# The last two products of the last output tile, computed in two halves of 128 columns, and another order of the last steps

## The chip, the cores and the metric

The kernel runs on one core of a Trainium2 chip. The metric is the device time of one execution in microseconds, and the number that counts is the median of several executions. Beside it stands one execution taken by the hardware profiler, on which all statements about single instructions rest. Engines are named as the profile names them: PE is the matrix engine, PEld its weight loads, DVE the vector engine, ACT the scalar engine, POOL the GpSimd engine, SP the sync engine, which here only issues DMAs and waits.

## The reference

The computation has two stages. The first is block-wise attention: a small 8x8 matrix per head is normalised by five rounds of exponential, row and column scaling, blocks of keys and values are mixed with it, and softmax attention runs inside each block of 96 positions. The second stage is a maxout layer over the 3072 tokens, and this is the one that the change touches:

```python
x  = attn_out.transpose(0, 2, 1, 3).reshape(B * S, H * D)   # 3072 x 512
h1 = x @ w1                                                  # 512 -> 1024
h2 = x @ w2
g  = maximum(h1, h2)
out = g @ w_out                                              # 1024 -> 512, float32
```

There are 4 batches of 768 tokens.

## The kernel before, in words

The kernel uses max(h1, h2) = relu(h1 - h2) + h2. So it computes g = relu(x(w1 - w2)) and then out = g w_out + x (w2 w_out), where w2 w_out is made once and kept as `wc`. The output product therefore contracts over 1024 rows of g and 512 rows of x, 12 blocks of 128 in all.

That output product is computed by the scheme that multiplies 2x2 blocks with seven products instead of eight. The two row blocks are the two halves of a batch (`ch` 0 and 1, 384 tokens each), the two column blocks are the two halves of the 512 output columns (`NW` = 256), and the two contraction blocks are the two halves of g and of x. Each of the seven products contracts over 6 blocks of 128. One class, `Group` (L932), holds what belongs together: a P group handles two tiles of 128 tokens of each half of the batch, a U group the third tile. A step of a P group is 12 matmuls of 128x128 weights by 256 columns, a step of a U group 6 of them.

The seven steps of a group (`step`, L1047, and `chain`, L1008) work on two banks of one PSUM buffer. Step 0 makes A11 B11 in bank 0 and copies it out. Step 1 makes A12 B21 in bank 1 and adds the copy: that is the first quarter of the output. Step 2 goes on adding to bank 0 and copies to the place of the quarter (ch 1, first columns); step 3 goes on in bank 0 and copies to the place of the quarter (ch 1, last columns); step 4 finishes bank 0 and copies it to the quarter (ch 0, last columns). Step 5 starts anew in bank 1 and adds its result to what step 3 left; step 6 goes on in the same bank 1 and adds to what step 2 left. `add` (L981) does a sum on DVE, `copy` (L992) a copy on DVE or ACT, `product` (L956) issues the matmuls, and `store` (L999) sends finished columns to the output. `send` (L1028) says what is stored after which step; after step 4 it is all of ch 0, after step 5 the last columns of ch 1, after step 6 of the last batch the first columns of ch 1, through ACT's queue.

Nothing here is scheduled by a planner. The order is a list of words written out by hand (L1176 to L1204), and each word is one step: `P3.5D` is step 5 of the P group of batch 3, with its sum on DVE, `U3.4A` step 4 of the U group with its copy on ACT, `O1.3.6` the store that follows step 6 of the U group (O0 is the P group). Each engine works through its own instructions in that order, and waits on counters (semaphores) for those of other engines. Reads of one bank do not hold up matmuls into the other bank, which `apart` (L941) declares.

DMAs issued by SP and ACT use eight completion semaphores in turn, numbered 0 to 7. At the end of the program SP waits for all of them, one instruction after another, in the order 0 to 7; then the engines meet at a barrier and the program ends. Before the change, the last store (`O1.3.6`, on ACT's queue) has semaphore 7, and SP's wait for it is the last of its nine.

Of the kernel before, what the change touches and what calls it, by code (L numbers as in the profile page):

```python
# [16 lines left out]
def kernel(  # L17
# [16 lines left out]
    nc = tc.nc  # L34
    AF = mybir.ActivationFunctionType
    ALU = mybir.AluOpType
    AX = mybir.AxisListType

    B, H, S, D = q.shape
# [14 lines left out]
    NW = DMODEL // 2  # L54
# [854 lines left out]
    def left(b, which, k, off):  # L909
        c = slice(off, off + 128)  # L910
        if k < 4:
            t, m = divmod(k, 2)
            if which in (1, 2, 4):
                return sums_g[:, {1: 0, 2: 1, 4: 2}[which], k, c]
            ch, t = {"a11": (0, t), "a12": (0, t + 2), "a22": (1, t + 2), 3: (1, t)}[which]
            return g_tiles[b, ch, t][:, m, c]
        j = k - 4
        if which in (1, 2, 3, 4):
            return sums_x[:, which - 1, j, c]
        ch, half = {"a11": (0, 0), "a12": (0, 1), "a22": (1, 1)}[which]  # L920
        return xT[:, b % 2, ch, j, half, c]

    def right(which, k):
        if which in (1, 2, 3, 4):
            if k >= 4:
                return wt_c[:, which - 1, k - 4]
            return (wt_early if which in (1, 3) else wt_late)[:, (which - 1) // 2, k]
        half, n = {"b11": (0, 0), "b21": (1, 0), "b22": (1, 1)}[which]
        n = slice(n * NW, (n + 1) * NW)
        return wo_sb[:, half * 4 + k, n] if k < 4 else wc[:, half * 2 + k - 4, n]  # L930

    class Group:  # L932
# [66 lines left out]
        def store(self, ch, c0=0, c1=DMODEL, queue=nc.sync):  # L999
# [5 lines left out]
                in_=self.o[ch][:, :, c0:c1],  # L1005
            )

        def chain(self, at, eng):  # L1008
            if at == 1:
                self.product(1, "a12", "b21", True)  # L1010
                self.add(0, 0, 1, self.by_tile(self.a), [self.first], eng)
            elif at == 2:
                self.product(0, 2, 2, False)
                self.second = self.copy(self.part(1, 0), 0, eng)
            elif at == 3:
                self.product(0, 1, 1, False)
                self.third = self.copy(self.part(1, 1), 0, eng)
            elif at == 4:
                self.product(0, 4, "b22", False)
                self.copy(self.part(0, 1), 0, eng)  # L1020
            elif at == 5:
                self.product(1, 3, 3, True)
                self.add(1, 1, 1, self.part(1, 1), [self.third], eng)
            else:
                self.product(1, "a22", 4, False)
                self.add(1, 0, 1, self.part(1, 0), [self.second], eng)

        def send(self, at):  # L1028

            last = self.b == B - 1  # L1030
            if at == 4:
                self.store(0)
            elif at == 5:
                self.store(1, NW)
            elif last:
                self.store(1, 0, NW, nc.scalar)
            elif len(self.tiles) > 1:
                self.store(1)
            else:
                nc.sync.dma_start(  # L1040
                    out=out[self.b * S : (self.b + 1) * S, :].rearrange(
                        "(c t p) n -> p c t n", c=2, p=128
                    )[:, :, self.tiles[0], :],
                    in_=self.both,
                )
# [35 lines left out]
    def token(text):  # L1081
# [117 lines left out]
        P2.3A x3.2 v3.6 U2.4D U2.6D x3.3 Y3.1.0D Y3.0.0D Y3.1.1D P2.5D P2.4A X3.1D X3.2D X3.3D P2.6D  # L1199
        Y3.0.2D Y3.1.2A X3.4D Y3.0.1D O1.2.6 Y3.0.3A O0.2.4 Y3.1.3D Y3.1.5A Y3.0.5D Y3.1.4A Y3.0.4A  # L1200
        Y3.1.6D Y3.0.6D U3.0A P3.0A G3.1.1D G3.0.1D G3.0.2D G3.1.2D O0.2.6 P3.1D G3.0.4D G3.0.3D
        G3.1.4D P3.2A G3.1.3D U3.1D U3.2A P3.3D P3.5D P3.4A P3.6D U3.3D U3.5D O0.3.5 O0.3.4 O0.3.6
        O1.3.5 U3.4A U3.6D O1.3.6 O1.3.4
        """,  # L1204
    ]
    for part in plan:
# [30 lines left out]
```

## Time and profile before

| what | us |
|---|---|
| median of 3 executions | 156.07 |
| lowest and highest | 155.84, 156.44 |
| the profiled execution's own time | 156.11 |
| its span, first to last instruction | 154.3 |
| outside the span | 1.8 |

The page of the profile gives busy times by engine, the span in 40 slices, the chain of work that ended last, the costliest groups of instructions and the DMAs. Where the text goes to single instructions it uses the timeline, whose rows give the start, the busy time from the first to the last of the merged instructions, engine, line, operation, output and inputs, shapes, and the count; the brackets at the end give the idle time of the engine before them and what ended it. A DMA that SP or ACT issues stands there with the time that the issue took; the time from issue to landing stands in the list of DMAs. The row of a group of matmuls ends when the last one has run through the array, which is later than the moment when the next matmul can start.

### The profile page before, as it was taken

How to read it: one execution, taken by the hardware profiler on the slowest of the kernel's cores; microseconds unless marked ns; L12 is line 12 of the kernel's file. 1: busy time of each engine (PE TensorE's matmuls, PEld its weight loads, DVE VectorE, ACT ScalarE, POOL GpSimd, SP SyncE). 2: the span in 40 equal slices, each digit the busy share in tenths (PEclk: the TensorE clock that was granted, in tenths of full speed). 3: DMA queues.
4: the chain of work that ended last, by engine and by line, in shares of the span. 5: the costliest groups of instructions: out<-in, count | busy, mean ns of one | idle time of the engine just before them, and what ended most of it. 6: DMA issues, size and time to landing. Idle time of an engine off the chain costs nothing.

```text
span 154.3 us, 5157 instructions
## 1 busy us (share of the span) xinstructions
PE 147.4 (96%) x2238; PEld 114.0 (74%) x2238; DVE 134.7 (87%) x287; ACT 102.0 (66%) x134; POOL 25.3 (16%) x53
## 2 busy tenths in 40 slices
PE   6999989999999999999999999989999999999991
PEld 6948867555678788887567998765688978578881
DVE  4888989999999999986999999658899999999731
ACT  3488897268899997879859797888792301463010
POOL 7999541100210400001500000000000000000000
PEclk9999999999999999999999999999999999999999
DMA  3999999999999972998999939996001475500065
GB/s 45 197 207 197 197 204 207 217 215 215 216 215 199 205 155 57 150 133 219 287 205 211 188 62 150 165 195 253 0 4 24 85 116 203 187 6 0 0 224 184
DMA packets 28918, 23.93 MB, mean 155 GB/s; under 512 B 16672, under 2 KB 24608, under 8 KB 28896
## 3 DMA queue, kind: packets, MB, share of 16 engines
q0 software_dynamic: 9280, 13.37, 49.1%
q1 hardware_dynamic: 19200, 9.84, 28.9%
q10 hardware_dynamic: 416, 0.39, 0.8%
q8 instruction: 17, 0.28, 0.7%
q14 instruction: 5, 0.04, 0.1%
HBM read 26.75 MB, written 6.29 MB: 214 GB/s over the span
## 4 chain that ended last, share of the span: by engine, by line
PE 62%; DVE 24%; ACT 4%; DMA 3%; issue 3%; DVEq 0%
PE out_ps L961 32%; PE hb_ps L805 10%; PE hq_ps L805 8%; PE o_ps L612 4%; DVE g L824 4%; DVE x L629 3%; PE k_ps L489 3%; PE s_ps L584 3%; DMA xT<-x 2%; ACT kT L109 2%; DVE w_sb L771 2%; PE v_ps L554 1%; DVE v_dc L255 1%; DVE sums_x L891 1%; DVE w_sb L236 1%
## 5 line engine op out<-in xcount | busy, mean ns | idle before, releaser
L805 PEld LDWEIGHTS <-w_sb 128*128 128x128 bf16 x224 | 21.5, 98 | 14.7 <-issue 0.8
L599 ACT ACTIVATE e<-s_ps 96x768 bf16<-96x768 f32 x32 | 24.1, 807 | 2.2 <-PE s_ps L584 2.0
L629 DVE TENSOR_TENSOR x<-o_ps,rs 96x512 bf16<-96x512 f32 x32 | 22.0, 686 | 1.1
L996 ACT COPY o<-out_ps 128x512 f32<-128x512 f32 (+1 forms) x18 | 8.6, 479 | 21.5 <-PE out_ps L961 21.2
L961 PEld LDWEIGHTS <-g 128*128 128x128 bf16 x192 | 18.2, 98 | 2.4
L805 PE MATMUL hb_ps<-sums_x,w_sb 128*128 128x384 bf16 x96 | 18.2, 327 | 0.0
L961 PEld LDWEIGHTS <-sums_g 128*128 128x128 bf16 x144 | 13.5, 97 | 2.2 <-issue 0.2
L961 PE MATMUL out_ps<-wo_sb,g 128*128 128x256 bf16 x96 | 13.1, 273 | 0.0
L987 DVE TENSOR_TENSOR o<-out_ps,o 128x512 f32<-128x512 f32 (+1 forms) x16 | 8.9, 553 | 4.7 <-PE out_ps L961 4.6
L109 ACT CAST kT<-k_ps 128x1024 bf16<-128x1024 f32 x12 | 11.6, 1020 | 2.0 <-PE k_ps L489 2.0
L805 PE MATMUL hq_ps<-xT,w_sb 128*128 128x384 bf16 x64 | 12.7, 326 | 0.0
L612 PE MATMUL o_ps<-v_sb,e 96*128 96x65 bf16 x256 | 12.4, 194 | 0.0
L612 PEld LDWEIGHTS <-e 96*128 96x128 bf16 x256 | 10.7, 98 | 1.5 <-DVE x L629 0.2
L961 PE MATMUL out_ps<-w2T,sums_x 128*128 128x256 bf16 x72 | 11.8, 273 | 0.0
L584 PE MATMUL s_ps<-qT,kT 64*128 64x96 bf16 x256 | 9.2, 204 | 1.1 <-ACT qT L109 0.7
L111 DVE CAST v_sb<-v_ps 96x1024 bf16<-96x1024 f32 x8 | 9.6, 1214 | 0.2 <-PE v_ps L531 0.2
L961 PEld LDWEIGHTS <-sums_x 128*128 128x128 bf16 x96 | 8.6, 97 | 1.2
L584 PEld LDWEIGHTS <-kT 64*128 64x128 bf16 x256 | 6.4, 94 | 3.5 <-issue 2.6
L826 ACT ACTIVATE g<-g 128x768 bf16<-128x768 bf16 x7 | 5.9, 842 | 4.4 <-DVE g L824 4.4
L83 PE MATMUL fill_ps<-fill 128*128 128x118 bf16 x92 | 7.3, 264 | 1.2 <-DVE fill L74 1.2
L176 POOL DMA_DIRECT2D v_raw<-in_v_dram x11 | 6.5, 597 | 11.2 <-DVE v_dc L255 4.3
L109 ACT CAST v_sb<-v_ps 96x1024 bf16<-96x1024 f32 x8 | 7.8, 1016 | 0.6 <-PE v_ps L554 0.6
(129 smaller groups left out, 304.2 us busy)
## 6 DMA issues: line engine op xcount, KB each, us to landing
out_dram<-o SPq DMA_DIRECT2D x10, 512.0 KB, 2.9
v_raw<-in_v_dram POOLq DMA_DIRECT2D x8, 384.0 KB, 16.2
k_raw<-in_k_dram POOLq DMA_DIRECT2D x3, 768.0 KB, 10.8
w_sb<-in_moe_w_dram POOLq DMA_DIRECT2D x4, 256.0 KB, 7.6
wo_sb<-in_moe_w_out_dram POOLq DMA_DIRECT2D x2, 512.0 KB, 11.2
w_sb<-in_moe_w_dram POOLq DMA_DIRECT2D x2, 512.0 KB, 14.8
v_raw<-in_v_dram POOLq DMA_DIRECT2D x3, 256.0 KB, 4.7
k_raw<-in_k_dram POOLq DMA_DIRECT2D x3, 256.0 KB, 6.4
```

The source lines that it names most:

```text
L83: nc.tensor.matmul(ps[:, 0:w], w0, fill[:, 0:w], start=True, stop=True)
L109: nc.scalar.copy(out=out_ap, in_=in_ap)
L111: nc.vector.tensor_copy(out=out_ap, in_=in_ap)
L176: nc.gpsimd.dma_start(out=v_raw[r0 : r0 + 64, m * n : (m + 1) * n], in_=v_src[b, :, m * n : (m + 1) * n],)
L584: nc.tensor.matmul(ps[:, h2 * 512 + ii * 128 : h2 * 512 + ii * 128 + BLK], kT[b][rows, (hp * 8 + i) * BLK : (hp * 8 + i) * BLK + 128], rhs ...
L599: nc.scalar.activation(out=e_out, in_=src, func=AF.Exp, scale=scale)
L612: nc.tensor.matmul(ps[:, h2 * 512 + ii * 65 : h2 * 512 + (ii + 1) * 65], e[:, (h2 * 4 + ii) * BLK : (h2 * 4 + ii) * BLK + 128], v_sb[:, m0 ...
L629: nc.vector.tensor_tensor(out=x, in0=ov[:, :, :, 0:D], in1=rs.to_broadcast([BLK, 2, 4, D]), op=ALU.mult,)
L805: nc.tensor.matmul(ps[:, m * 512 : m * 512 + TCH], w[:, k, c : c + 128], x[:, k], start=new and k == 0, stop=k == 1, skip_group_check=True,)
L961: ins = nc.tensor.matmul(self.ps[:, bank * 512 + p * NW : bank * 512 + (p + 1) * NW], left(self.b, lw, k, ti * 128), right(rw, k), start=n ...
L987: ins = nc.vector.tensor_tensor(out=self.part(ch, half), in0=self.by_tile(self.bank(n)), in1=other, op=ALU.add)
L996: ins = nc.scalar.copy(out=out, in_=self.by_tile(self.bank(n)))
```

## The change

For the last batch's U group alone, steps 5 and 6 go through a new function `halves`: the 256 columns are made as two halves of 128. The first half goes to bank 0, the second to bank 1, in step 5 and in step 6, and each half has its own sum on DVE. Step 6 still goes on adding to what step 5 left in the same bank. The store after step 6 is cut into two of 128 columns: the first on SP's queue, the second on ACT's. The last steps stand in another order: steps 3 and 4 of the U group move ahead of steps 6 and 4 of the P group, and steps 5 and 6 of the U group now follow each other at the very end, right after step 6 of the P group. The stores move with them. Over the whole program there is one DMA more on SP's queue, so that the last store on ACT's queue has semaphore 0 instead of 7.

```diff
+        def halves(self, at):
+
+            lw, rw, need, c0 = (3, 3, self.third, NW) if at == 5 else ("a22", 4, self.second, 0)
+            for h in range(2):
+                c = slice(h * 128, h * 128 + 128)
+                bank = self.ps[:, h * 512 : h * 512 + 128]
+                for n, k in enumerate(self.ks):
+                    ins = nc.tensor.matmul(
+                        bank,
+                        left(self.b, lw, k, self.tiles[0] * 128),
+                        right(rw, k)[:, c],
+                        start=at == 5 and n == 0,
+                        stop=n == len(self.ks) - 1,
+                        skip_group_check=True,
+                    )
+                    self.apart(ins, h)
+                to = self.o[1][:, 0, c0 + h * 128 : c0 + h * 128 + 128]
+                self.read(
+                    nc.vector.tensor_tensor(out=to, in0=bank, in1=to, op=ALU.add), h, [need]
+                )
+
         def chain(self, at, eng):
-            if at == 1:
+            if at > 4 and self.b == B - 1 and len(self.tiles) == 1:
+                self.halves(at)
+            elif at == 1:
...
             elif at == 5:
                 self.store(1, NW)
+            elif last and len(self.tiles) == 1:
+                self.store(1, 0, 128)
+                self.store(1, 128, NW, nc.scalar)
             elif last:
                 self.store(1, 0, NW, nc.scalar)
...
-        G3.1.4D P3.2A G3.1.3D U3.1D U3.2A P3.3D P3.5D P3.4A P3.6D U3.3D U3.5D O0.3.5 O0.3.4 O0.3.6
-        O1.3.5 U3.4A U3.6D O1.3.6 O1.3.4
+        G3.1.4D P3.2A G3.1.3D U3.1D U3.2A P3.3D P3.5D U3.3D P3.4A U3.4A O0.3.5 P3.6D O0.3.4
+        O1.3.4 U3.5D O0.3.6 O1.3.5 U3.6D O1.3.6
```

## The prediction

> **What bounds the kernel now.** I read the page's busy times first, then the chain of work that ended last, from 130 us on, and then the timeline of the last ten microseconds, because the change touches nothing before them.
>
> ```profile
> PE 147.4 (96%) x2238; PEld 114.0 (74%) x2238; DVE 134.7 (87%) x287; ACT 102.0 (66%) x134; POOL 25.3 (16%) x53
> ...
> 137.23 13.95 PE out_ps L961 x126
> 151.18 0.02 issue
> 151.21 0.42 DVE o L987
> ```
>
> PE is busy all the time, and the chain that ended last is PE without a gap up to 151.2, one sum on DVE, and then what follows it: the last store and the end of the program. So a change in the last steps is worth what it moves of three things: the moment at which the last sum on DVE ends, the time for which the last store flies, and what follows its landing.
>
> ```profile
> 145.67 0.60 PE L961 MATMUL out_ps<-wc,sums_x 128*128 128x256 bf16 x4
> ...
> 147.42 1.04 PE L961 MATMUL out_ps<-w2T,g 128*128 128x256 bf16 x8
> 148.29 0.38 PE L961 MATMUL out_ps<-w2T,sums_x 128*128 128x256 bf16 x2
> ...
> 148.50 0.69 DVE L987 TENSOR_TENSOR o<-out_ps,o 128x512 f32<-128x512 f32 x1 [1.93 <-PE out_ps L961]
> ...
> 149.22 0.42 DVE L994 COPY o<-out_ps 128x256 f32<-128x256 f32 x1
> 149.50 0.30 PEld L961 LDWEIGHTS <-sums_x 128*128 128x128 bf16 x2
> 149.70 0.38 PE L961 MATMUL out_ps<-wc,sums_x 128*128 128x256 bf16 x2
> ...
> 150.57 0.60 PE L961 MATMUL out_ps<-w2T,g 128*128 128x256 bf16 x4
> 151.21 0.42 DVE L987 TENSOR_TENSOR o<-out_ps,o 128x256 f32<-128x256 f32 x1 [0.97 <-PE out_ps L961]
> 151.66 0.35 ACTq L1001 DMA_DIRECT2D out_dram<-o  x1
> ```
>
> In these rows P's step 4 starts at 145.67, P's step 6 ends in the array at 147.42 + 1.04 = 148.46, and its sum on DVE takes 0.69 from 148.50. U's steps 3 and 5 follow, then a short stall (U's step 4 waits until 149.70 for the copy on DVE that ends at 149.64), then U's steps 4 and 6. The last sum ends at 151.21 + 0.42 = 151.63 and the last store is issued at 151.66. The next rows are the DMA list of the last ten microseconds, SP's waits after 151.3, and SP's closing waits that had nothing to wait for.
>
> ```profile
> out_dram<-o SPq DMA_DIRECT2D x2, 256.0 KB, 2.1
> out_dram<-o SPq DMA_DIRECT2D x1, 512.0 KB, 2.8
> ...
> out_dram<-o ACTq DMA_DIRECT2D x1, 128.0 KB, 1.7
> ```
>
> ```profile
> SPq L1232 <- DMA out_dram<-o: 1.6, 3, 1.0
> ```
>
> ```profile
> L1232 SPq EVENT_SEMAPHORE  x6: 28/28/28, 151.3 to 151.6; - x6
> ```
>
> The last store lands 1.7 after its issue, at 153.4, and 0.9 of closing work follows it inside the span of 154.3. Six closing waits that were already met took five steps from 151.3 to 151.6, that is about 0.06 each. That small price matters below.
>
> **The change part by part.** The instruction order of the changed program shows, on DVE, the sequence: sum of P's step 5, copy of U's step 3, sum of P's step 6, then the four half sums; on PE the first half of U's step 6 waits for the first half sum of step 5, and the second half for the second.
>
> *PE's order.* The 24 matmuls from 145.67 to 148.29 start 2.62 / 24 = 0.109 apart. In the new order U's step 3 (6 matmuls) starts at 145.67, P's step 4 at 146.33, U's step 4 at 147.64, P's step 6 at 148.29 and U's step 5 at 149.60. U's step 4 now finds its copy ready: U's step 3 leaves the array near 146.5, DVE comes free then from the sum of P's step 5, and the copy takes 0.42, to about 147.0. So the old stall goes: 149.70 - 149.50 = 0.20 between two starts where 0.11 is usual, 0.09 saved.
>
> *Half-width matmuls.* The change makes 24 matmuls of 128 columns out of 12 of 256. The trace has such a run with fresh weights for each:
>
> ```profile
> 18.85 0.61 PE L675 MATMUL tw_ps<-ident,w_sb 128*128 128x128 bf16 x8
> ```
> ```profile
> L675 PE MATMUL tw_ps<-ident,w_sb 128*128 128x128 bf16 x32 | 2.5, 220 | 0.0
> ```
>
> One takes 0.22 to leave the array, so eight start (0.61 - 0.22) / 7 = 0.056 apart, and a half of 6 takes 0.33. The two halves of step 5 then run from 149.60 to 150.27. All 24 cost 24 x 0.056 = 1.34 against 12 x 0.109 = 1.31, next to nothing. Here the Trainium skill's page "TensorE: Matmul & The Clock Gate" (section "Back-to-back issue gap") speaks against the change: for a stream of weight load and matmul pairs it gives a measured 81 ns a matmul at 128 columns. By that figure the sum below would be 0.3 higher; the row above disagrees with it.
>
> *What is late next: DVE.* P's step 6 starts its last matmul at 149.49 and it leaves the array 0.27 later, at 149.77 (the matmul rows of this line have a mean of 273 ns). Its sum on DVE runs from 149.81 to 150.50, and the half sums of U's step 5 queue behind it. A half sum is not in the trace; the nearest rows are a sum out of PSUM of 64 columns and the one of 256 above:
>
> ```profile
> L384 DVE TENSOR_TENSOR pm<-pe,maskJ 128x64 f32<-128x64 f32 x1 | 0.2, 218 | 0.0
> ...
> L987 DVE TENSOR_TENSOR o<-out_ps,o 128x256 f32<-128x256 f32 x2 | 0.8, 425 | 1.1 <-PE out_ps L961 1.1
> ```
>
> Between 0.22 and 0.42, on the line through both, 128 columns take 0.29. So the first half sum runs from 150.53 (DVE took 0.03 between 149.19 and 149.22) to 150.82. PE, which had nothing else to do from 150.27, starts the first half of step 6 at 150.87 (0.05 after DVE, as at 149.64 and 149.70): a new stall of 0.6. Behind the waiting matmul on PE stands all of step 6, and for that wait the last two sums and both last stores. The second half starts at 151.20, its second-half partner from step 5 having ended near 151.11, starts its last matmul at 151.48 and leaves the array at 151.70; the sum runs from 151.74 to 152.03. Against 151.63 that is **+0.40**. The first half of step 6 is summed from 151.4 to 151.7, in time.
>
> *Handing over to the last store.* Before, ACT's last store waits for DVE directly and starts 0.03 after it. Now a separate wait instruction stands ahead of it, since the store waits for two semaphores. Bounds are 0 and 0.1; a wait of ACT on DVE for the copy that ended at 149.64 is at 149.7 and takes 17 ns:
>
> ```profile
> L996 ACTq EVENT_SEMAPHORE  x1: 17/17/17, 149.7 to 149.7; - x1
> ```
>
> I take **+0.05**, so the last store is issued at 152.11.
>
> *The last store.* It has 64 KB, in 128 rows of 512 bytes. Landings of 2.8, 2.1 and 1.7 for 512, 256 and 128 KB shrink by 0.7 and 0.4; the next halving would give 0.2. The other bound is nothing, because 8 KB (a load) took as long as 128 KB:
>
> ```profile
> p_sb<-in_sort_net_dram SPq DMA_DIRECT2D x1, 8.0 KB, 1.7
> ```
>
> I take **-0.15**, nearer the stores. Other stores don't disturb it: U's ch 0 store now leaves near 148.9, P's last one at 150.5, U's last columns at 151.1 and the first half store at 151.75, each with its landing time over before the last one moves data (about 153).
>
> *After the landing.* Before, the last store has the last of SP's closing waits. Now it has semaphore 0, the second of nine, so seven waits, all met by then, still follow its landing: 7 x 0.06 = **+0.42**. Before, they ran while the store was in flight.
>
> *The sum.* 0.40 + 0.05 - 0.15 + 0.42 = +0.72. The profiled execution's 156.11 (span 154.3, 1.8 around it) becomes 156.83; from the median, 0.04 below it, 156.79. I predict **156.8**, 0.5% above before, just inside the 0.78 that is 0.5%, about what a measurement of this kernel can tell from no change.
>
> PE's clock is granted in full to the end, so the stall needs no term for it:
>
> ```profile
> 150.00:151.20 1.20, 1.17 (x11) 0.79 (x9) 0.23 (x1) 0.37 (x1) 0.00 (x0) 1.00 0.78 256
> ```
>
> **The rivals.**
> - *Slower by more than 0.5%: the smaller store is not quicker.* Its landing is a fixed flight, the same for 8 and 128 KB by the two rows with 1.7. Place: the last store; price 0.15 back; it decides from a saving under 0.09 on, since 0.87 without it is over 0.78. Time 157.0. Against it speak the shrinking landings of the stores.
> - *Closing waits are free.* If SP passes them while the last store is in flight, +0.42 goes: +0.30, 156.4. Against it: they are single instructions of SP in a fixed order, and before SP stood 1.0 in one of them.
> - *DVE does not hold PE up*, the change's halves overlapping as laid out. Then PE runs on at 150.27, but DVE still has 0.69 and four half sums in a row: 150.53 + 4 x 0.29 = 151.69, only 0.06 after before instead of 0.40. Sum +0.38, 156.5. Against it: the wait is in the program, and P's sum cannot start before its product is done.
> - *Slow half-width matmuls.* At 81 ns step 5 still hides behind P's sum, step 6 does not: 12 x 0.025 = 0.3 more, 157.1. This is the rule of the page cited above; the row of 32 matmuls speaks against it.
>
> No single one makes it faster: even without DVE's hold and without the closing waits the sum is 0.06 + 0.05 - 0.15 = -0.04.
>
> **How the numbers follow.** The forecast has 0.48, split 0.26 within and 0.22 above 0.5%, since it lies at that line. The small store without gain has 0.24 (0.19 slower, 0.05 within), free closing waits 0.08 and no hold by DVE 0.07 (both within), slow matmuls 0.06, a collision of stores at the end that I have not seen 0.04 (both slower), faster for a reason not found 0.03. Faster 0.03, within 0.5% 0.46, slower 0.51. The forecast's own range is 156.6 to 157.0. The range of 156.35 to 157.15 takes in the bounds of the store, of the handover and of the half sums (2 x 0.07 either way), and the rivals' times.
>
> **What would show it.** In the new profile: U's step 4 without a stall; PE idle about 0.6 between steps 5 and 6 of U, released by DVE; half sums of about 0.29, the last ending 0.4 later than before; the last store landing in 1.5 to 1.6; and after its landing seven closing waits, with about 1.3 instead of 0.9 to the end of the span. A last half sum that ends before 151.8, or a last landing followed by only 0.9, would make the forecast wrong.

## The result, and the profile after

| | median us | lowest and highest | runs |
|---|---|---|---|
| before | 156.01 | 155.26, 157.80 | 10 |
| changed | 156.84 | 156.55, 157.62 | 10 |

The changed kernel takes 1.0066 times as long, with a 95% interval of 1.0044 to 1.0088. It was timed once more beside the experiments: 156.65 against 155.99, ratio 1.0028, 0.9996 to 1.0060, an interval that includes 1. Medians are over all executions, ratios and their intervals leave out the few that fell into a slower state of the chip, and a ratio is not the quotient of the two medians beside it. 156.8 had been forecast. The profiled execution of the changed kernel took 156.71, with a span of 154.9 against 154.3.

The first view is the page's line of busy times of the changed kernel, and the end of its chain of work that ended last.

```profile
PE 146.8 (95%) x2247; PEld 113.6 (73%) x2250; DVE 134.6 (87%) x289; ACT 102.0 (66%) x134; POOL 25.7 (17%) x53
```
```profile
139.98 9.76 PE out_ps L961 x89
149.74 0.02 issue
149.76 0.36 DVE o L987
150.12 0.25 issue
150.37 0.29 DVE o L1026
150.66 0.04 issue
150.70 0.84 PE out_ps L1015 x12
151.55 0.02 issue
151.57 0.29 DVE o L1026
```

Before, the chain was PE without a break until 151.2 and one sum. Now it leaves PE at 149.74, goes through two sums on DVE, and comes back to PE at 150.70 for the 12 matmuls of U's step 6. The timeline shows the same stretch (start, busy time, engine, line, operation, shapes, count, and in brackets the idle time and what ended it):

```profile
147.59 0.38 PE L961 MATMUL out_ps<-wc,sums_x 128*128 128x256 bf16 x2
...
149.56 0.28 PE L1015 MATMUL out_ps<-w2T,sums_x 128*128 128x128 bf16 x2
...
149.76 0.69 DVE L987 TENSOR_TENSOR o<-out_ps,o 128x512 f32<-128x512 f32 x1 [2.78 <-PE out_ps L961]
...
150.00 0.39 PE L1015 MATMUL out_ps<-wt_early,g 128*128 128x128 bf16 x4
...
150.37 0.48 DVE L1026 TENSOR_TENSOR o<-out_ps,o 128x128 f32<-128x128 f32 x2
...
150.70 0.27 PE L1015 MATMUL out_ps<-w2T,xT 128*128 128x128 bf16 x2 [0.31 <-DVE o L1026]
...
151.15 0.39 PE L1015 MATMUL out_ps<-w2T,g 128*128 128x128 bf16 x4
151.23 0.62 DVE L1026 TENSOR_TENSOR o<-out_ps,o 128x128 f32<-128x128 f32 x2 [0.39 <-PE out_ps L1015]
```

U's step 4 (147.59) and step 5 (149.56) start without an idle time of PE ahead of them. U's step 5 leaves the array at 150.39, PE is idle for 0.31, and DVE's first half sum releases it. The last half sum ends at 151.23 + 0.62 = 151.85. The next rows are the last stores of the changed kernel (KB and median time from issue to landing), SP's waits after 151.8, and SP's closing waits after the landing.

```profile
out_dram<-o ACTq DMA_DIRECT2D x1, 256.0 KB, 2.3
out_dram<-o SPq DMA_DIRECT2D x1, 128.0 KB, 2.2
out_dram<-o SPq DMA_DIRECT2D x1, 64.0 KB, 1.8
out_dram<-o ACTq DMA_DIRECT2D x1, 64.0 KB, 1.6
```
```profile
SPq L1258 <- DMA out_dram<-o: 1.6, 1, 1.6
```
```profile
L1258 SPq EVENT_SEMAPHORE  x8: 28/28/28, 153.6 to 154.0; - x8
```

Before, SP stood in three closing waits for stores one after another. Now it stands 1.6 in one, that for semaphore 0, and when the last store has landed at 153.6, that wait and seven more pass from 153.6 to 154.0.

Executions differ ahead of the last steps: the sum of P's step 5 starts between 145.7 and 146.8 in the profiles of this study, although no kernel differs from the others before 125 us. So the profiles are compared from the start of that sum on. All times of this table are from the traces, in us after that start:

| kernel | last sum ends | last store issued | it lands | end of span |
|---|---|---|---|---|
| before | 5.76 | 5.79 | 7.52 | 8.42 |
| changed | 6.03 | 6.12 | 7.75 | 9.08 |
| e1, before with one store more | 5.75 | 5.78 | 7.51 | 8.84 |
| e2, changed, semaphore 7 | 6.03 | 6.12 | 7.74 | 8.67 |
| e3, changed without P's last sum | 5.84 | 5.87 | 7.69 | 9.02 |
| e4, the order alone | 6.34 | 6.37 | 8.10 | 9.02 |
| e5, e3 without P's last store | 5.84 | 5.93 | 7.52 | 8.88 |
| e6, U's step 5 ahead of P's step 6 | 6.31 | 6.49 | 8.67 | 9.57 |
| e7, halves in a buffer of their own | 5.64 | 5.72 | 7.35 | 8.26 |
| e8, changed again | 6.03 | 6.12 | 7.75 | 9.10 |

The change costs 9.08 - 8.42 = 0.66 in these last nine microseconds: 0.27 until the last sum, 0.06 until the store's issue, -0.10 in its flight and 0.43 after it. Each row of the table is one execution; the two of the changed kernel (changed and e8) agree to 0.02 in every column.

### The profile page after: what moved, and what is told of

Read it like the earlier page. It is cut to its first block, busy times and chain, and to the rows that moved or that the text cites. A ratio compares the mean times of both kernels' runs of the same rounds, so it can differ in the third digit from the quotient of the medians.

```text
span 154.9 us, 5183 instructions
## 1 busy us (share of the span) xinstructions
PE 146.8 (95%) x2247; PEld 113.6 (73%) x2250; DVE 134.6 (87%) x289; ACT 102.0 (66%) x134; POOL 25.7 (17%) x53
## 4 chain that ended last, share of the span: by engine, by line
PE 55%; DVE 18%; DMA 16%; ACT 5%; issue 3%; POOL 0%; DVEq 0%
PE out_ps L961 31%; DMA v_raw<-in_v_dram 12%; PE hb_ps L805 7%; DVE g L824 5%; PE hq_ps L805 5%; PE o_ps L612 4%; PE k_ps L489 3%; DMA xT<-x 3%; PE s_ps L584 2%; ACT kT L109 2%; PE v_ps L554 1%; DVE sums_x L891 1%; DVE g L828 1%; DVE v_dc L255 1%; DVE sums_g L907 1%
## 5 line engine op out<-in xcount | busy, mean ns | idle before, releaser
L961 PEld LDWEIGHTS <-g 128*128 128x128 bf16 x184 | 17.4, 98 | 2.4
L987 DVE TENSOR_TENSOR o<-out_ps,o 128x512 f32<-128x512 f32 (+1 forms) x14 | 8.0, 571 | 4.4 <-PE out_ps L961 4.3
L250 ACT COPY v_dc<-v_raw 64x1152 bf16<-64x1152 bf16 (+3 forms) x6 | 8.2, 1380 | 0.0
```

Source lines behind the costliest of these rows:

```text
L250: nc.scalar.copy(out=dst.rearrange("p (d c two) -> p d c two", c=BLK, two=2)[:, :, c0:c1], in_=src.rearrange("p (c d two) -> p d c two", c ...
L961: ins = nc.tensor.matmul(self.ps[:, bank * 512 + p * NW : bank * 512 + (p + 1) * NW], left(self.b, lw, k, ti * 128), right(rw, k), start=n ...
L987: ins = nc.vector.tensor_tensor(out=self.part(ch, half), in0=self.by_tile(self.bank(n)), in1=other, op=ALU.add)
```

## The experiments

The theory under test was that of the prediction: PE's wait for DVE, a slower handover, a slightly faster store, and seven closing waits. The chief rivals were that the loss after the landing has nothing to do with the semaphore's number, and that PE waits for its own half sums and not for the P group's sum. The timings below lie too close to one another to tell most of these kernels apart; what each run shows is read from its trace.

**e1: one store more, 25 us before the end.**

```diff
-            if at == 4:
+            if at == 4 and self.b == 2:
+                self.store(0, 0, NW)
+                self.store(0, NW)
+            elif at == 4:
                 self.store(0)
```

> The kernel before, with one store of batch 2 (after step 4 of its P group, some 25 us before the end) cut into two, so that the last store of all gets semaphore 0 instead of 7. Theory (SP's closing waits after the landing cost about 0.06 each, and seven of them now follow the last landing): the span is 0.4 longer than before, all of it between the landing of the last store and the end; chain up to the last store unchanged. Rival (the closing waits are passed while the store flies, or cost nothing): same span as before, within 0.1.

Its last sum, store and landing are those of before to 0.01. After the landing the kernel takes 1.33 instead of 0.90, so the end comes 0.42 later. SP's closing waits, one standing for 2.0 and eight passing in half a microsecond, are these:

```profile
SPq L1235 <- DMA out_dram<-o: 2.0, 1, 2.0
```
```profile
L1235 SPq EVENT_SEMAPHORE  x8: 28/28/28, 154.3 to 154.8; - x8
```

Its whole span was 155.7, not 154.7, because this execution was 0.9 late already at the sum of P's step 5. In the timed runs it took 156.62 against 156.10, ratio 1.0021 (0.9994 to 1.0049), which 0.42 us (0.27%) fits, though no change would fit as well. A store that nobody waited for, long before the end, thus costs 0.4 us through the number of a semaphore.

**e2: the changed kernel with the old semaphore.**

```diff
             if at == 4:
-                self.store(0)
+                self.store(0, queue=nc.gpsimd if self.b == 2 else nc.sync)
```

> The changed kernel, with that same store of batch 2 issued on the queue of POOL instead of SP's, so that the last store of all gets semaphore 7 again. Theory: 0.43 of the change's loss goes, the span falls from 154.9 to about 154.5, the last landing stays at 153.6 and 0.9 instead of 1.3 follow it. Rival (the loss after the landing comes from something else in the last steps): 154.9 again.

Everything up to the landing is as in the changed kernel; 0.93 follow it instead of 1.33, and the end comes at 8.67 instead of 9.08. After 153.5 only two closing waits of SP are left before it goes on, the last at 153.8:

```profile
L1258 SPq EVENT_SEMAPHORE  x2: 28/28/28, 153.5 to 153.8; - x2
```

Timed: 156.38 against 156.10, ratio 1.0004 (0.9978 to 1.0030). With e1 this shows the closing term from both sides. The other traces agree: in the table, from the last landing to the end it is 1.33 to 1.36 in the five kernels whose last store has semaphore 0 (changed, e1, e3, e5, e8) and 0.90 to 0.93 in the five in which it has 7.

**e3: without the P group's last sum.**

```diff
                 self.product(1, "a22", 4, False)
-                self.add(1, 0, 1, self.part(1, 0), [self.second], eng)
+                if eng == "A":
+                    self.copy(self.part(1, 0), 1, eng)
+                else:
+                    self.add(1, 0, 1, self.part(1, 0), [self.second], eng)
...
-        ... U3.4A O0.3.5 P3.6D O0.3.4
+        ... U3.4A O0.3.5 P3.6A O0.3.4
```

> The changed kernel, with step 6 of the last P group only copied on ACT instead of summed on DVE: the addition of what step 2 left is left out of one quarter of two tiles. Theory (the sum of the P group's step 6 holds DVE when U's half sums become due, and so holds PE): the first half sum starts at about 150.1 instead of 150.4, PE's stall of 0.3 to 0.5 shrinks to about 0.2, the last half sum ends at 151.6 instead of 151.86, span 154.6 to 154.7. Rival (PE would wait anyway, for the half sums themselves): the last half sum still ends at 151.8 to 151.9, span 154.9.

The half sums come forward as expected, but by 0.19 and not by 0.26: the last one ends 5.84 after the mark.

```profile
146.06 0.69 DVE L987 TENSOR_TENSOR o<-out_ps,o 128x512 f32<-128x512 f32 x1 [0.56 <-PE out_ps L961]
...
150.39 0.56 DVE L1026 TENSOR_TENSOR o<-out_ps,o 128x128 f32<-128x128 f32 x2 [3.19 <-PE out_ps L1015]
151.27 0.63 DVE L1026 TENSOR_TENSOR o<-out_ps,o 128x128 f32<-128x128 f32 x2 [0.32 <-PE out_ps L1015]
```
```profile
150.23 0.39 PE L1015 MATMUL out_ps<-wt_early,g 128*128 128x128 bf16 x4
150.74 0.27 PE L1015 MATMUL out_ps<-w2T,xT 128*128 128x128 bf16 x2
```

DVE now waits for PE (3.19 idle) ahead of the first half sum, so the P group's sum did hold it up. PE's idle time between U's steps 5 and 6 falls from 0.31 to 0.12 (150.23 + 0.39 = 150.62 to 150.74) and does not vanish: for that part the rival is right too: PE also waits for its own first half sum, which ends at 150.68. Of the 0.27 that the last sum came later, the P group's sum thus has 0.19. The other 0.08 (5.84 against 5.76 before) is a balance: the wait for the own half sum, less what the smaller last sum and the vanished stall of U's step 4 save. But the span hardly gained: 9.02 against 9.08, because the last two stores flew longer (first and second half below), the last one 1.8 instead of 1.6. Timed: 156.67 against 156.10, ratio 1.0028 (1.0001 to 1.0056).

```profile
out_dram<-o SPq DMA_DIRECT2D x1, 64.0 KB, 1.9
out_dram<-o ACTq DMA_DIRECT2D x1, 64.0 KB, 1.8
```

**e4: the order alone.**

```diff
-            if at > 4 and self.b == B - 1 and len(self.tiles) == 1:
-                self.halves(at)
-            elif at == 1:
+            if at == 1:
...
             elif last and len(self.tiles) == 1:
-                self.store(1, 0, 128)
-                self.store(1, 128, NW, nc.scalar)
+                self.store(1, 0, NW, nc.scalar)
```

> The changed kernel without the halves: the new order of the last steps alone, steps 5 and 6 of U whole in one bank, and one last store (semaphore 7). Theory (the order is what costs, because it puts U's step 6 right behind its step 5, whose sum it waits for, and the halves win a part back): last sum ends near 152.1 against 151.63 before and 151.86 with halves; last store lands after 1.7; no extra closing waits; span about 154.8, 0.5 above before. Rival (the halves are what costs): the last sum ends at 151.7 or earlier and the span is that of before, 154.3.

```profile
145.88 0.69 DVE L987 TENSOR_TENSOR o<-out_ps,o 128x512 f32<-128x512 f32 x1 [0.56 <-PE out_ps L961]
...
149.81 1.08 DVE L987 TENSOR_TENSOR o<-out_ps,o 128x512 f32<-128x512 f32 x2 [2.78 <-PE out_ps L961]
151.79 0.42 DVE L987 TENSOR_TENSOR o<-out_ps,o 128x256 f32<-128x256 f32 x1 [0.91 <-PE out_ps L961]
```
```profile
150.94 0.38 PE L961 MATMUL out_ps<-w2T,xT 128*128 128x256 bf16 x2 [0.52 <-DVE o L987]
```

Here PE is idle for 0.52, and the last sum ends at 152.21, 6.34 after the mark. The end comes 0.60 later than before, by the order alone; 0.5 was expected. So the order is what costs. The halves win 0.31 back at the last sum and 0.10 in the store's flight, and lose 0.06 at the handover and 0.41 through the additional store: in all they cost 0.06 (9.08 against 9.02). Timed: 156.89 against 156.10, ratio 1.0032 (1.0004 to 1.0060).

**e5: e3 without the P group's last store.**

```diff
-            if at == 4:
+            if at == 4 and self.b == 2:
+                self.store(0, 0, NW)
+                self.store(0, NW)
+            elif at == 4:
                 self.store(0)
...
-        O1.3.4 U3.5D O0.3.6 O1.3.5 U3.6D O1.3.6
+        O1.3.4 U3.5D O1.3.5 U3.6D O1.3.6
```

> As the kernel without the P group's last sum, and also without that group's last store (256 KB, so a quarter of two tiles of batch 3 is not written); one store of batch 2 is cut in two, so that the last store keeps semaphore 0. Times from the start of the sum of P's step 5, because runs differ ahead of it. Theory (in the run without the sum, the earlier end of the last half sum was eaten because the last stores follow each other too closely, behind the P group's store): the last half sum ends 5.84 after, as without the sum, but the last store lands in 1.6 instead of 1.81, and the end comes 8.8 after, 0.2 sooner. Rival (1.81 is chance, or the two halves alone are in each other's way): 1.8 again, end 9.0 after.

```profile
out_dram<-o SPq DMA_DIRECT2D x1, 128.0 KB, 1.7
out_dram<-o SPq DMA_DIRECT2D x1, 64.0 KB, 1.6
out_dram<-o ACTq DMA_DIRECT2D x1, 64.0 KB, 1.6
```

The last sum ends at 5.84 as in e3, and all three last stores are fast again; U's last columns (128 KB) land after 1.7 instead of 2.3. The end comes at 8.88 instead of 9.02, though the store itself was issued 0.05 later here. So the 256 KB of the P group, issued in the changed kernel's order 1.3 later than before, stand ahead of the other stores in the DMA engines; the rows by queue under the last heading show it. The kernel was executed once, in 156.36.

**e6: U's step 5 ahead of P's step 6.**

```diff
-        ... U3.4A O0.3.5 P3.6D O0.3.4
-        O1.3.4 U3.5D O0.3.6 O1.3.5 U3.6D O1.3.6
+        ... U3.4A O0.3.5 U3.5D P3.6D O0.3.4
+        O1.3.4 O1.3.5 O0.3.6 U3.6D O1.3.6
```

(and the store of e2 on POOL's queue.)

> The changed kernel with U's step 5 moved ahead of P's step 6, and semaphore 7 for the last store (one store of batch 2 on POOL's queue). Everything is computed. Theory (PE's stall comes from having U's step 6 right behind its step 5; with 12 matmuls between, it goes, and then DVE's row of P's sum and two half sums sets the end): no stall on PE, the last half sum ends 5.7 after the start of the sum of P's step 5 (changed kernel 6.03, before 5.76), but the P group's store leaves 0.6 later and the last store lands in 1.8 instead of 1.63; end 8.5 after (changed 9.08, before 8.42). Rival (the stores at the end do not hold each other up): landing 1.6, end 8.3.

```profile
148.94 0.27 PE L1015 MATMUL out_ps<-w2T,sums_x 128*128 128x128 bf16 x2 [0.46 <-ACT o L996]
...
150.92 0.28 PE L1015 MATMUL out_ps<-w2T,xT 128*128 128x128 bf16 x2
```
```profile
out_dram<-o ACTq DMA_DIRECT2D x1, 256.0 KB, 2.5
out_dram<-o SPq DMA_DIRECT2D x1, 128.0 KB, 2.1
out_dram<-o SPq DMA_DIRECT2D x1, 64.0 KB, 2.1
out_dram<-o ACTq DMA_DIRECT2D x1, 64.0 KB, 2.2
```

This expectation missed. The stall between steps 5 and 6 is gone as expected, but another appeared ahead of step 5: its first half goes into bank 0, which step 4 has just used, and ACT's copy of step 4 must have read it. In the changed kernel the 12 matmuls of P's step 6 cover that copy; here PE is idle for 0.46. Everything after it is late, the last sum ends at 6.31, and the last store, issued right behind the P group's, lands after 2.2. The end is 9.57, although semaphore 7 saves 0.42. Timed: 157.36 against 155.99, ratio 1.0069 (1.0036 to 1.0101).

**e7: the old order, with the halves in a buffer of their own.**

```diff
+            if at == 5:
+                self.half_ps = ps_f32("half_ps")
...
-                bank = self.ps[:, h * 512 : h * 512 + 128]
+                bank = self.half_ps[:, h * 512 : h * 512 + 128]
...
-            if at == 4:
-                self.store(0)
+            if at == 1:
+                self.store(0, 0, NW)
+            elif at == 4 and self.b == B - 1 and len(self.tiles) == 1:
+                self.store(0, NW)
+            elif at == 4:
+                self.store(0, queue=nc.gpsimd if self.b == 2 else nc.sync)
...
-                self.store(1)
+                self.store(1, queue=nc.gpsimd if self.b == 2 else nc.sync)
...
-        ... U3.1D U3.2A P3.3D P3.5D U3.3D P3.4A U3.4A O0.3.5 P3.6D O0.3.4
-        O1.3.4 U3.5D O0.3.6 O1.3.5 U3.6D O1.3.6
+        ... U3.1D U3.2A O1.3.1 P3.3D P3.5D P3.4A P3.6D U3.3D U3.5D O0.3.5 O0.3.4 O0.3.6
+        O1.3.5 U3.4A O1.3.4 U3.6D O1.3.6
```

> An attempt to beat both: the order of before, with steps 5 and 6 of U in two halves in a PSUM buffer of their own (so that step 4 can stand between them), the first quarter of U's output stored as soon as it is ready, and two stores of batch 2 on POOL's queue so that the last store has semaphore 7. Theory (with the sums hidden behind step 4, the halves win what a smaller last sum and store are worth): PE's stall of the change is gone, the last half sum ends 5.6 after the start of the sum of P's step 5 (before 5.76), the last store lands in 1.6, end 8.25 after, 0.15 to 0.2 sooner than before; in the timed runs no more than 0.1%, that is, same. Rival (stores hold each other up here too): landing 1.8, end 8.4, as before.

```profile
146.34 0.69 DVE L987 TENSOR_TENSOR o<-out_ps,o 128x512 f32<-128x512 f32 x1 [0.56 <-PE out_ps L961]
...
150.21 0.49 DVE L1028 TENSOR_TENSOR o<-half_ps,o 128x128 f32<-128x128 f32 x2
151.35 0.63 DVE L1028 TENSOR_TENSOR o<-half_ps,o 128x128 f32<-128x128 f32 x2 [0.65 <-PE half_ps L1017]
```

With step 4 between steps 5 and 6 again, the halves do what a smaller last sum and store can: the last sum ends at 5.64, the store lands after 1.63 and the end comes at 8.26, 0.16 sooner than before. That is 0.1%, and the timed runs can't tell it from nothing: 155.86 against 155.99, ratio 0.9993 (0.9964 to 1.0021). By the trace it is the shortest ending of all, and by the times the same as before.

**e8: the changed kernel again.**

> The changed kernel once more, on the same chip and beside the same runs of before as the others. By the profile the change costs 0.6 to 0.7 us, 0.4%; the timed runs gave 0.66% with an interval of 0.44 to 0.88. Theory (all of the loss is in the last 9 us): the profile again shows an end 9.08 after the start of the sum of P's step 5, and the ratio is 1.004. Rival (something ahead of the last steps got slower too): the ratio stays at 1.006 or above and the sum of P's step 5 starts later than in before, run for run.

The end comes at 9.10, and the ratio is 1.0028. Its interval holds 1.0042, which 0.66 of 156 makes; that of the first timing begins just above, at 1.0044, so the first timing shows slightly more than the trace accounts for. The rival is not borne out: the sum of P's step 5 starts at 145.98 here and at 145.83 in the first trace of the changed kernel, on either side of the 145.88 of before. With one or two traces of each kernel a small loss ahead of the last steps is not ruled out.

## Why the prediction came out right

- *PE's order* held: P's step 6 and both halves of U's step 5 run without a stall, and U's step 4 no longer waits.
- *Half-width matmuls* held: the half steps' matmuls follow each other in the same 0.056 as the row of before had it (four with 0.22 to leave the array take 0.39). The 81 ns that the Trainium skill's page "TensorE: Matmul & The Clock Gate" gives for such streams (section "Back-to-back issue gap") did not appear, and that rival falls.
- *PE waits for DVE* held, and e3 and e4 show it. Its size was wrong: +0.40 was expected, +0.27 measured. The prediction's stall of 0.6 counts from the moment when the next matmul could start; counted so, the changed kernel has 150.70 - (150.00 + 4 x 0.056) = 0.48, and 0.31 is the idle time of the row. The mis-sized term is the row of sums on DVE, which the prediction set one behind the other, 0.03 apart. In fact the first half sum starts at 150.37, while the P group's sum runs until 149.76 + 0.69 = 150.45, and two half sums of 0.28 take 0.48 together. Starting 0.08 before the end of the sum ahead instead of 0.03 after it makes 0.11 of the missing 0.13.
- *Handover*: +0.05 expected, +0.06 measured.
- *The last store*: -0.15 expected, -0.10 measured. That other stores don't disturb each other was wrong for the two ahead of it (2.2 for 128 KB, 1.8 for the first half), but hardly touched the last one, as 1.63 here and 1.60 in e5 show. So the rival of a small store without any gain falls too.
- *After the landing*: +0.42 expected, +0.43 measured, and shown by e1 and e2. That closing waits are free falls.
- *The sum*: 0.72 expected, 0.66 in the trace; the medians differ by 0.83 and 0.66 in the two timings. The mechanism of every term is borne out, and all sizes but that of the wait for DVE come within 0.05; that the first median, 156.84, came within 0.04 of the forecast is partly luck, as the two timings of the same change differ by more than that.

The traces also show where one execution falls behind another ahead of the last steps. From 105 us to the mark every one keeps its distance from before to within 0.02 us (e1 +0.94, e7 +0.46, e8 +0.11, changed -0.05), and no edit acts before 125 us. Up to 105 us the chain of work waits for DMAs of different length, first in before, then in e1:

```profile
98.80 3.65 DMA xT<-x
```
```profile
74.13 8.90 DMA k_raw<-in_k_dram
...
99.50 3.89 DMA xT<-x
```

In e1 the chain waits until 83.03 for a load of keys, which the chain of before does not have between 70 and 98 us, and the transposing DMA of x stands in it for 0.24 longer. Why these landings vary stays open.

## What to carry to other kernels

At the end of a kernel, look for the step whose result the next step on the same accumulator must wait for, and keep independent work between the two: the order cost 0.6 us here, and cutting the work into halves won back 0.4, which the additional store cost again. The order must not open another wait elsewhere, as e6 did. Look also at what follows the last landing: closing waits stand in a fixed order, and one DMA more on the queues of SP or ACT, even 25 us before the end, can move the last store from the end of that order to its beginning. And when stores are all pushed to the end, an earlier last sum can bring little: in e3 it ended 0.19 earlier, and the last store landed 0.06 earlier.

## What the runs showed of the hardware

Closing waits of SP that are already met follow each other about 0.06 us apart (eight from 153.6 to 154.0 in the changed kernel), and only after the wait ahead of them has been met.

In the changed kernel a half sum that queues on DVE behind another sum, with its matmuls done 0.3 us before, starts 0.08 us before the recorded end of the one ahead (150.37 against 150.45). A copy that queues behind a sum starts 0.03 after its end (149.22 against 148.50 + 0.69 = 149.19 in before). No run here shows what makes the difference.

What a store has to wait for can be read from the stretch of 0.75 us that begins 5.62 after the mark, first in the changed kernel, then in e5 without the P group's last store (columns: stretch, length, busy time and count of PE, PEld, DVE, ACT, POOL, PE's granted clock, DMA share, GB/s; below it packets, MB and share of the queue that moves the data):

```profile
151.45:152.20 0.75, 0.08 (x2) 0.00 (x0) 0.37 (x2) 0.00 (x0) 0.00 (x0) 1.00 0.98 326
...
q10 hardware_dynamic: 239, 0.24, 97.6%
```
```profile
151.28:152.03 0.75, 0.00 (x0) 0.00 (x0) 0.22 (x1) 0.00 (x0) 0.00 (x0) 1.00 0.54 177
...
q1 hardware_dynamic: 149, 0.13, 53.6%
```

q10 is ACT's queue: in the whole kernel before it moves 0.39 MB, which ACT's two stores of 256 KB and 128 KB make. In the changed kernel the P group's store of 256 KB has the DMA engines to itself here (97.6%), although the store of 128 KB on SP's queue was issued before the stretch began; that one lands after 2.2 us. In e5 the same stretch moves the 128 KB, and they land after 1.7.
